# Attention: two places for the halves of normalised tiles and finished heads and for the output sum, and the heads' halves made one step later

## The chip, the cores and the metric

The kernel runs on one core of one Trainium2 chip. A core has a matrix engine (TensorE, PE in the profile; PEld are its weight loads), a vector engine (VectorE, DVE), a scalar engine (ScalarE, ACT), GpSimd (POOL) and a synchronisation engine (SyncE, SP), which issues every DMA of this kernel. Each engine works through its own queue in order and waits at semaphores for the others. SBUF is the on-chip memory of 128 partitions; addresses below are bytes within a partition. PSUM holds the sums of matmuls.

The metric is the device time of one execution in microseconds (us). A profiled execution gives the trace; its own time is given beside its span, which runs from the first to the last instruction.

## The reference

Two layers of a mixed network on a sequence of S = 2048 rows of D = 640. Each layer is an attention with a compressive memory followed by a gated mixing over the sequence; the same weights serve both layers.

```python
def A(x, wq, wk, wv, wo, beta):          # H = 32 heads of 20, N = 4 segments of 512 rows
    q, k, v = heads(x @ wq), heads(x @ wk), heads(x @ wv)
    for s in range(N):
        p = softmax(q[s] @ k[s].T * scale + causal_mask)
        a_mem = (phi(q[s]) @ M) / (phi(q[s]) @ z + 1e-6)
        o[s] = g * a_mem + (1 - g) * (p @ v[s])
        M, z = M + phi(k[s]).T @ v[s], z + phi(k[s]).sum()
    return concat(o) @ wo

def B(x, w_in, w_sp, b_sp, w_out):       # F = 1728
    z = gelu(x @ w_in); z1, z2 = z[:, :864], layernorm(z[:, 864:])
    return (z1 * (w_sp @ z2 + b_sp)) @ w_out

for _ in range(2):
    x = x + A(layernorm(x), ...)
    x = x + B(layernorm(x), ...)
```

## The kernel before

**Stages.** Per layer the kernel runs an attention (phase1a, class Attention), the projection into B with the rest of the attention's output projection (phase1b, "w_in stage"), and the mixing with the output projection of B (phase2 in the first layer, phase2s in the second). Every matmul works on halves: a float32 value is kept as a 16-bit high half and a 16-bit low half (the difference), and a product is three matmuls, high by high, high by low, low by high. Making halves is a copy on ScalarE for the high one and a subtraction for the low one.

**The attention in steps.** Heads are taken in 64 pairs per layer (16 per segment of 512 rows), and a pair takes three steps, c = 0, 1, 2. In a step PE computes a part of the scores of pair n (tile es, whose exponential on ScalarE is P) and of the transposed scores of pair n + 2 (tile mp, whose maxima on VectorE are mx). The casts that halve P (PH on ScalarE, PL on GpSimd, in the last four pairs partly on VectorE) are made in the steps c = 2 and c = 0, one head each, and the products of P with the values (pv) follow three steps later. combine, in a step c = 1, scales pv (rs, ab on VectorE) and adds its parts on GpSimd (oat). The maxima, turned by PE (mtp) and halved (mr), go by DMA into the rows of qk that the scores of a later step read. Between these steps PE works off "dense" jobs in a written order with paces: values (vps), queries and keys (qps, kps), and the output projection of finished tiles (yps).

post(k, f) runs f in the step k further on; that fixes where f's instructions stand in the program, and with it their priority.

**Finished heads.** Each segment has five units m of 6 or 8 heads. When the last pair of a unit has been combined, out() halves its 4 x 6 x 20 (or 4 x 8 x 20) columns: a copy on ScalarE (L1368), a subtraction on GpSimd (L1369), and two DMAs into o_d in DRAM (L1372). load_o brings such rows back transposed for project, and an assertion keeps its step behind the segment's last out().

**Normalised tiles.** prep loads a tile of x, normalises it in place (L1044), and halves and transposes it by DMA (split_t: L231 copy, L232 subtraction on GpSimd, L233 DMA transpose into xt). Its halves, named xnhl, take the same tag "xh" of the pool e1 as the heads' halves, named ohl: one place for both.

**The output sum.** project multiplies a transposed tile of heads by wo in two halves of 320 columns; for each, VectorE adds x and writes the sum x1 (L1104), and after the second the tile is stored (L1106). x1 has one place, tag "xn" of the pool e1. Twelve tiles a layer (0 to 11) go through project inside the attention, the last ones at its very end; tiles 12 to 15 are left to phase1b.

**Phase 1b** begins while the attention ends. For its first two tiles it loads x1 (L275), normalises it (tile xn, L225, after layernorm_stats), and halves and transposes it (tile xnhl, L231 to L233) into th, which the w_in matmuls (zp, L316) take. Tile i's matmuls with the second half of w_in come first, then those with the first half (wi0 in the first layer, loaded raw through the stages wst, L123, and split into wi0h and wi0l, L84 and L85; loaded ready in the second). xn and xnhl have one place each.

**Order.** Only PE's order is the program's own (manual_schedule). The other queues, SP's too, are laid out when the kernel is built, by a planner that simulates a timeline and takes the ready instruction of the highest priority.

**Memory.** Pools of one side are stacked in the order in which they are opened, and a later pool takes the bytes of an earlier one that has ended. With reuse_waits="tile" a tile in such a place waits only for those earlier tiles that held its own bytes, and for a tile that a DMA reads until that DMA has landed. In the program before, a partition is used as follows.

| bytes | the attention (left side) | first layer's phase1b, same bytes | second layer's phase1b (right side) |
|---|---|---|---|
| 83840-148288 | qk, vs, P, PH, PL, ot, gm, ab and others | zh, zl, z1, z2 | zb (left) |
| 148288-150848 | xh: xnhl and ohl (pool e1) | z2, xt | |
| 150848-153408 | xn: x1 (pool e1) | xt | o |
| 153408-158528 | xt, two places (e2) | xt, o, wst | o |
| 158528-163648 | bg, two places | wst | o, xt |
| 163648-171840 | phq, four places (u4) | wst, x1, th | xt, z2, zt |
| 171840-182080 | xt1 (ax) | th, xn, xnhl 176896-179456, wi0h from 179456 | z2, zt, z1 |
| 182080-182656 | small tiles, mr (al1); in the second layer mr alone, to 182592 | wi0h to 188096 | z1 to 183904 |
| above | free | wi0l 188096-196736 | xn 183904-186464, xnhl 186464-189024, x1, th to 199264 |

The pools of the attention that the change touches are opened in setup:

```python
sk, self.p3, self.pl2 = pool("ak", 1), pool("a3", 2), pool("al2", 2)
self.e1, self.e2, self.bg, self.u4, ax = pool("ae1", 1), pool("ae2", 2), pool("abg", 2), pool("au4", 4), pool("ax", 1)
self.pl1 = pool("al1", 1)
```

phase2 makes the first tiles of the second layer's attention ahead of it, with pools of its own under the same names (nxt.e2, nxt.e1).

Of the kernel before, what the change touches and what calls it, by code (L numbers as in the profile page):

```python
# [9 lines left out]
F32 = mybir.dt.float32  # L10
F32R = mybir.dt.float32r
F16 = mybir.dt.float16
# [7 lines left out]
S, D, H, DH, NSEG = 2048, 640, 32, 20, 4  # L20
# [606 lines left out]
def phase2(g, w_sp, x1_d, z1_d, zh, zl, out, nxt):  # L627
# [5 lines left out]
    with ExitStack() as ctx:  # L633
        pool = lambda n, b, **k: ctx.enter_context(tc.tile_pool(name=n, bufs=b, reuse_waits="tile", **k))
        right = lambda n, b: pool(n, b, side="right")
        p1, pr, ph0, ph1, p2, wp = pool("c1", 1), pool("cr", 1), pool("ch0", 1), pool("ch1", 1), pool("c2", 2), pool("cw", 1)
        sp, pt1, px, pt0 = right("cs", 3), right("ctr1", 1), right("cx", 1), right("ctr0", 1)
        nxt.e2, nxt.e1 = pool("ce2", 1), pool("ce1", 1)
        pg = pool("cg", 2, space=PSUM)
        py = pool("cy", 1, space=PSUM)  # L640
        nxt.pd = pool("cpd", 2, space=PSUM)
# [45 lines left out]
        def fetch(nm, src):  # L687
            o = p2.tile([128, src.shape[-1]], F32, tag=nm, name="c" + nm)
            nc.sync.dma_start(o, src)
            return o  # L690
# [54 lines left out]
        for t in range(NT):  # L745
# [8 lines left out]
            x1 = fetch("x1", x1_d[t])  # L754
# [102 lines left out]
def values_tile(g, pool):  # L857
    t = pool.tile([128, 4, H, 2 * DH + 1], F16, name="vs")
    g.nc.gpsimd.memset(t[:, :, :, DH:DH + 1], 1.0)
    return t  # L860
# [9 lines left out]
class Attention:  # L870
# [56 lines left out]
    def setup(self, ctx):  # L927
        g, nc, tc = self.g, self.nc, self.tc
        pool = lambda n, b, **k: ctx.enter_context(tc.tile_pool(name=n, bufs=b, reuse_waits="tile", **k))
        sk, self.p3, self.pl2 = pool("ak", 1), pool("a3", 2), pool("al2", 2)  # L930
        self.e1, self.e2, self.bg, self.u4, ax = pool("ae1", 1), pool("ae2", 2), pool("abg", 2), pool("au4", 4), pool("ax", 1)
        self.pl1 = pool("al1", 1)
        self.pd = pool("apd", 2, space=PSUM)
        self.px = pool("apx", 1, space=PSUM)
        self.pm = pool("apm", 1, space=PSUM)
        self.pe = pool("ape", 1, space=PSUM)
        self.po = pool("apo", 1, space=PSUM)
        self.qk = [sk.tile([128, 2, L], F16, name=f"qk{i}") for i in range(self.NQK)]
        self.vs[1] = values_tile(g, sk)
        self.xt[1] = ax.tile([128, 2, KD, L], F16, name="xt1")  # L940
# [90 lines left out]
    def prep(self, t, lead=False):  # L1031

        g, nc = self.g, self.nc
        s, c = t // 4, slice((t % 4) * 128, (t % 4) * 128 + 128)
        xt = self.e2.tile([128, D], F32, tag="xt", name="xt")
        nc.sync.dma_start(xt, self.x[t])
        ln = []

        def stats():
            ln.extend(layernorm_stats(g, xt, D, 2, XS))  # L1040

        def norm():
            mv, rs = ln
            nc.vector.tensor_scalar(xt, xt, mv[:, 0:1], rs, ALU.subtract, ALU.mult)  # L1044
            hl = self.e1.tile([128, 2, D], F16, tag="xh", name="xnhl")
            split_t(g, hl, self.xt[s % 2][:, :, :, c], xt, low=nc.gpsimd)

        def held(f):
            with self.tc.high_priority(offset=HP) if lead else self.hold():
                f()  # L1050

        return lambda: held(stats), lambda: held(norm)
# [30 lines left out]
    def project(self, t):  # L1083
        g, nc = self.g, self.nc
        wh, wl = g.wo.h, g.wo.l
        o = self.o.pop(t)
        oh, ol = o[:, 0], o[:, 1]
        xt = self.e2.tile([128, D], F32, tag="xt", name="xt")
        nc.sync.dma_start(xt, self.x[t])
        x1 = self.e1.tile([128, D], F32, tag="xn", name="x1")  # L1090
        yield 450
        for n in range(2):
            c = slice(n * 320, (n + 1) * 320)
            ps = self.pd.tile([128, L], F32, tag="dn", name="yps")[:, :320]
            i = 0
            for k in range(KD):
                for a, b in ((oh, wh), (oh, wl), (ol, wh)):
                    nc.tensor.matmul(ps, a[:, k, :], b[:, k, c], start=(i == 0), stop=(i == 14))  # L1098
                    i += 1
                    if i % 3 == 0:  # L1100
                        yield 3 * 136

            def out(ps=ps, c=c, n=n):
                nc.vector.scalar_tensor_tensor(x1[:, c], ps, g.yw, xt[:, c], ALU.mult, ALU.add)  # L1104
                if n:
                    nc.sync.dma_start(self.x1_d[t], x1)  # L1106

            self.post(1, out)
# [236 lines left out]
    def combine(self, n, s, m, h0):  # L1345
# [17 lines left out]

        def out():
            nh = len(UH[m])
            hl = self.e1.tile([128, 2, D], F16, tag="xh", name="ohl")[:, :, :4 * nh * DH].rearrange("p i (t h d) -> p i t h d", t=4, d=DH)
            oh, ol = hl[:, 0], hl[:, 1]
            nc.scalar.copy(oh, ot[:, :, :nh, :])  # L1368
            nc.gpsimd.tensor_tensor(ol, ot[:, :, :nh, :], oh, ALU.subtract)  # L1369
            c = slice(UH[m][0] * DH, (UH[m][0] + nh) * DH)  # L1370
            for i, o in enumerate((oh, ol)):
                nc.sync.dma_start(self.o_d[s][:, i, c].rearrange("(t p) c -> p t c", p=128), o.rearrange("p t h d -> p t (h d)"))  # L1372

        self.post(2, out)

    def run(self, nseg=NSEG):
        pairs = [(s, m, h0) for s in range(nseg) for m in range(NU) for h0 in UH[m][::2]]
# [227 lines left out]
```

## Time and profile before

| | us |
|---|---|
| median of three runs | 2323.73 (2322.91 to 2328.16) |
| the profiled execution's own time | 2331.88 |
| its span | 2330.2 |

By stages of the profiled execution (us from the start of the span; busy us of each engine):

| stage | from | to | PE | DVE | ACT | POOL | granted clock |
|---|---|---|---|---|---|---|---|
| start, first weights and tiles | 0 | 150 | 99.95 | 108.63 | 62.92 | 43.38 | 0.93 |
| first attention | 150 | 650 | 450.41 | 392.76 | 385.46 | 404.09 | 0.96 |
| into the w_in stage | 650 | 676 | 16.53 | 10.71 | 9.78 | 1.06 | 0.80 |
| w_in stage | 676 | 897 | 220.77 | 108.17 | 65.98 | 17.79 | 1.00 |
| mixing, first layer | 897 | 1250 | 352.89 | 158.48 | 71.75 | 13.68 | 1.00 |
| into the second attention | 1250 | 1300 | 44.87 | 29.57 | 18.23 | 6.11 | 0.97 |
| second attention | 1300 | 1790 | 457.42 | 385.28 | 396.44 | 422.62 | 0.99 |
| w_in stage | 1790 | 1983 | 191.79 | 130.84 | 71.99 | 59.94 | 1.00 |
| mixing, second layer | 1983 | 2330 | 338.85 | 178.94 | 91.78 | 2.85 | 1.00 |

How to read the lines of the profile: a group has line, engine, operation, tiles as out<-in, count, then busy us, mean ns of one, idle us of the engine just before them and what ended that idle time. A line of the timeline has start and duration in us, engine, line, operation and tiles, a count, and in brackets the idle time before it with its releaser. SPq is SP's queue at the issue of a DMA. A line of waits has the waiting instruction, what it waited for, us in total, times, and the longest. A line of windows has the stretch, its length, the busy time of PE, PEld, DVE, ACT and POOL with the number of instructions, the granted clock of PE, the share of the DMA engines that was busy, and GB/s.

### The profile page before, as it was taken

To read this page: it belongs to the slowest core of one execution; us is meant where nothing else is said; L and a number is where in the kernel's file an instruction comes from. 1 tells how busy PE (TensorE), PEld (TensorE's weight loads), DVE (VectorE), ACT (ScalarE), POOL (GpSimd) and SP (SyncE) were. 2 spreads that over 40 slices of the span, in tenths; PEclk is the share of its full clock that TensorE was granted. 3 is DMA by queue.
4 is the path that set the end of the run, shared out by engine and by line. 5 is a ranking of instruction groups with operands and counts; after the bars stand their busy time and mean duration, and the time that the engine had idled before them with its cause. 6 is when DMAs were issued, how large, how long until landed. Compare 5 with 4: busy or idle time off the path is not lost.

```text
span 2330.2 us, 50381 instructions
## 1 busy us (share of the span) xinstructions
PE 2173.5 (93%) x20490; PEld 1297.3 (56%) x20490; DVE 1503.4 (65%) x2791; ACT 1174.3 (50%) x1452; POOL 971.5 (42%) x726
## 2 busy tenths in 40 slices
PE   4878899899889999999999989999998999999998
PEld 2445465556645555555655555656665555555655
DVE  8678868877644545454434788787776757555454
ACT  3279778787632232122212797887875324322221
POOL 2178778888710000000001688888895323000000
PEclk9999899999999999999999999999999999999999
DMA  5654544544563457878655336354466434977875
GB/s 162 166 138 102 131 107 128 129 144 117 146 168 90 132 160 196 244 189 243 162 144 157 75 92 181 103 125 95 122 170 166 116 102 102 264 205 188 227 200 124
DMA packets 509561, 350.16 MB, mean 150 GB/s; under 512 B 409296, under 2 KB 444496, under 8 KB 504208
## 3 DMA queue, kind: packets, MB, share of 16 engines
q1 hardware_dynamic: 509328, 346.93, 56.4%
q8 instruction: 161, 2.64, 0.5%
q14 instruction: 72, 0.59, 0.1%
HBM read 160.83 MB, written 97.93 MB: 111 GB/s over the span
## 4 chain that ended last, share of the span: by engine, by line
PE 65%; DVE 11%; DMA 8%; ACT 7%; issue 3%; SPq 1%; POOL 1%; ACTq 0%; DVEq 0%; POOLq 0%
PE zp L316 14%; PE gp L683 10%; PE pv L1341 4%; PE cyp L715 3%; PE yps L1098 3%; PE cyp L519 3%; DVE mx L1304 3%; PE ga L469 3%; PE mp L1288 3%; PE kps L1122 3%; ACT P L1297 2%; PE qps L1122 2%; PE vps L1065 2%; PE gb L469 2%; ACT PH L1314 2%
## 5 line engine op out<-in xcount | busy, mean ns | idle before, releaser
L1315 POOL TENSOR_TENSOR PL<-P,PH 128x1280 f16<-128x1280 f32 x248 | 649.5, 2621 | 167.8 <-ACT PH L1314 154.7
L1304 DVE TENSOR_REDUCE mx<-mp 128x2 f32<-128x1024 f32 (+3 forms) x512 | 408.8, 818 | 97.2 <-PE mp L1260 95.6
L1297 ACT ACTIVATE P<-es,sc 128x1024 f32<-128x1024 f32 (+1 forms) x384 | 370.3, 964 | 135.3 <-PE es L1260 133.2
L1314 ACT CAST PH<-P 128x1280 f16<-128x1280 f32 x256 | 320.4, 1253 | 21.6 <-PE pv L1341 12.9
L219 POOL TENSOR_TENSOR lnrs<-lnve,mhalf 128x1 f32<-128x1 f32 x92 | 56.1, 618 | 576.2 <-DVE lnve L218 576.2
L316 PEld LDWEIGHTS <-th 128*128 128x128 f16 x1920 | 188.5, 98 | 177.2 <-issue 16.4
L683 PE MATMUL gp<-zh,wt 128*128 128x432 f16 x1024 | 231.4, 346 | 0.3 <-DMA wt<-wn 0.3
L683 PEld LDWEIGHTS <-wt 128*128 128x128 f16 x1536 | 150.1, 98 | 129.8 <-DMA wt<-wn 1.1
L1288 PEld LDWEIGHTS <-qk 60*128 60x128 f16 (+1 forms) x2048 | 91.1, 93 | 225.8 <-issue 154.3
L469 PEld LDWEIGHTS <-wt 128*128 128x128 f16 x1344 | 131.5, 98 | 112.6
L1288 PE MATMUL mp<-qk 60*128 60x512 f16 (+3 forms) x1024 | 138.2, 307 | 41.1 <-DVE mx L1304 40.1
L1341 PE MATMUL pv<-vs,PH 128*128 128x41 f16 x2560 | 168.6, 183 | 2.1 <-DVE ab L1357 2.0
L1260 PEld LDWEIGHTS <-big 64*128 64x128 f16 x3072 | 141.5, 96 | 50.9 <-issue 3.9
L1341 PE MATMUL pv<-vs,PL 128*128 128x41 f16 x2560 | 164.4, 182 | 4.4 <-POOL PL L1315 3.9
L1288 PE MATMUL es<-qk 64*128 64x512 f16 (+3 forms) x1024 | 135.7, 300 | 35.0 <-ACT P L1297 25.4
L1065 PE MATMUL vps<-wvh,xt 128*128 128x320 f16 x640 | 151.5, 302 | 3.6 <-DVE vs L1071 3.0
L1341 PEld LDWEIGHTS <-PH 128*128 128x128 f16 x2560 | 142.9, 96 | 18.7
L316 PE MATMUL zp<-wi1h,th 128*128 128x432 f16 x640 | 149.2, 348 | 2.1 <-DVE x L1104 1.3
L1341 PEld LDWEIGHTS <-PL 128*128 128x128 f16 x2560 | 143.4, 97 | 7.8 <-POOL PL L1315 4.7
L683 PE MATMUL gp<-zl,wt 128*128 128x432 f16 x512 | 135.3, 346 | 0.0
L1122 PE MATMUL kps<-xt,wkh 128*128 128x512 f16 x380 | 124.0, 395 | 9.1 <-DVE phl L1156 9.0
L696 DVE TENSOR_TENSOR u<-u,cz 128x864 f32<-128x864 f32 x16 | 17.0, 1060 | 160.8 <-ACT u L694 120.4
(253 smaller groups left out, 4386.2 us busy)
## 6 DMA issues: line engine op xcount, KB each, us to landing
wr<-in_B_w_sp_dram SPq DMA_DIRECT2D x32, 1024.0 KB
qk<-st SPq DMA_DIRECT2D x256, 120.0 KB
x<-x SPq DMA_DIRECT2D x56, 320.0 KB
z<-z SPq DMA_DIRECT2D x32, 432.0 KB
cz<-z SPq DMA_DIRECT2D x32, 432.0 KB
turned<-wt SPq DMA_DIRECT2D x24, 512.0 KB
wt<-turned SPq DMA_DIRECT2D x24, 512.0 KB
st<-qhl SPq DMA_DIRECT2D x40, 256.0 KB
```

The lines of the kernel that those rows point to most:

```text
L316: nc.tensor.matmul(zp[:, n, :FHH], a[:, k, :], b[:, k, c:c + FHH], start=(k == 0 and j == 0), stop=(k == KD - 1 and j == 2))
L469: nc.tensor.matmul(o[:, :FHH], wt[:, x, m, :], zb[b][:, y, m, :], start=start and i == j == 0, stop=i == NP - 1 and j == 2, skip_group_che ...
L683: nc.tensor.matmul(gp[:, n, :FHH], ready[t][:, k % 2, a, k // 2, :], b[:, k, n * FHH:(n + 1) * FHH], start=(i == 0 and j == 0), stop=(i == ...
L1065: nc.tensor.matmul(ps, a[:, k, c], b[:, k, n * 320:(n + 1) * 320], start=(i == 0), stop=(i == 14))
L1122: nc.tensor.matmul(ps, a[:, k, c], b[:, k, :], start=(i == 0), stop=(i == 14))
L1260: nc.tensor.matmul(out, g.big[r, 64 - 64 * s:192 - 64 * s], mk, start=False, stop=s == 1, skip_group_check=True)
L1288: nc.tensor.matmul(out[:, h, o:o + w], a[r, ac], b[r, bc], start=o == 0, stop=False, skip_group_check=True)
L1297: self.last_of["ACT"] = nc.scalar.activation(P[:, :, 512 * c:512 * c + ew], es[:, :, :ew], AF.Exp, scale=g.esc).ins
L1304: self.last_of["DVE"] = nc.vector.tensor_reduce(self.mx[m][:, :, i], mp[:, :, o:o + w], AX.X, ALU.max).ins
L1314: nc.scalar.copy(PH, P[:, h])
L1315: (nc.gpsimd if h == 0 or n < self.N - self.TAIL else nc.vector).tensor_tensor(PL, P[:, h], PH, ALU.subtract)
L1341: nc.tensor.matmul(pv[:, i, h, :], x[:, c:c + 128], v[:, j, h0 + h, :], start=(j == 0 and x is PH), stop=(j == i and x is PL), skip_group_ ...
```

## The change

The pool e1 of one place goes. The halves of normalised tiles and of finished heads get a pool axh of two places, still shared by both, and the output sum x1 gets a pool axn of two places; both are opened last, behind al1. In phase2 the pool of one place that prep uses there gets the new name. The halves of finished heads are posted three steps on instead of two, but for the last pair of the layer, which keeps two.

```diff
-        nxt.e2, nxt.e1 = pool("ce2", 1), pool("ce1", 1)
+        nxt.e2, nxt.xh = pool("ce2", 1), pool("ce1", 1)
...
-        self.e1, self.e2, self.bg, self.u4, ax = pool("ae1", 1), pool("ae2", 2), pool("abg", 2), pool("au4", 4), pool("ax", 1)
-        self.pl1 = pool("al1", 1)
+        self.e2, self.bg, self.u4, ax = pool("ae2", 2), pool("abg", 2), pool("au4", 4), pool("ax", 1)
+        self.pl1, self.xh, self.xn = pool("al1", 1), pool("axh", 2), pool("axn", 2)
...
-            hl = self.e1.tile([128, 2, D], F16, tag="xh", name="xnhl")
+            hl = self.xh.tile([128, 2, D], F16, tag="xh", name="xnhl")
...
-        x1 = self.e1.tile([128, D], F32, tag="xn", name="x1")
+        x1 = self.xn.tile([128, D], F32, tag="xn", name="x1")
...
-            hl = self.e1.tile([128, 2, D], F16, tag="xh", name="ohl")[:, :, :4 * nh * DH].rearrange("p i (t h d) -> p i t h d", t=4, d=DH)
+            hl = self.xh.tile([128, 2, D], F16, tag="xh", name="ohl")[:, :, :4 * nh * DH].rearrange("p i (t h d) -> p i t h d", t=4, d=DH)
...
-        self.post(2, out)
+        self.post(2 if n + 1 == self.N else 3, out)
```

A place of either tag is 2560 bytes (2 x 640 values of 16 bits, or 640 of 32 bits).

## The prediction

> **What bounds the kernel now.** The page comes first, then the waits of TensorE (PE) in each attention stage, then the stages' windows.
>
> ```profile
> span 2330.2 us, 50381 instructions
> PE 2173.5 (93%) x20490; PEld 1297.3 (56%) x20490; DVE 1503.4 (65%) x2791; ACT 1174.3 (50%) x1452; POOL 971.5 (42%) x726
> PE es L1288 <- ACT P L1297: 11.6, 9, 3.5
> PE es L1288 <- DMA qk<-mr: 4.5, 3, 2.1
> PE pv L1341 <- POOL PL L1315: 1.6, 3, 1.1
> PE es L1288 <- ACT P L1297: 11.7, 16, 1.8
> PE es L1288 <- DMA qk<-mr: 4.0, 4, 1.7
> 1790.00:1983.00 193.00, 191.79 (x1081) 105.69 (x1081) 130.84 (x227) 71.99 (x104) 59.94 (x62) 1.00 0.44 118
> ```
>
> PE is the bound: 93% of the span, and 191.8 of 193 us in the w_in stage behind the second attention (1790 to 1983). Its order is written out, so a hole in PE is lost unless a later hole shrinks by it. The three rows of waits from 150 to 650 us and the two from 1300 to 1780 us (us, times, longest) say what this change can touch: 11.6 + 11.7 = 23.3 us for ScalarE's P, 8.5 us for the maxima's DMA. VectorE's maxima make longer holes; the change leaves them.
>
> **What it does in the attention.** Halves of normalised tiles (xnhl) and of finished heads (ohl) share one place now, so each waits for the other's DMA.
>
> ```profile
>   DMA xt<-xnhl: 9.4, 6
>   DMA xt<-xnhl: 12.7, 5
> L1369 POOL TENSOR_TENSOR ohl<-oat,ohl x40: 1091/1098/1403, 152.8 to 1789.5; 128x480 f16<-128x480 f32 x32, 128x640 f16<-128x640 f32 x8
> 413.29 0.72 ACT L1368 CAST ohl<-oat 128x640 f16<-128x640 f32 x1 [1.88 <-DMA xt<-xnhl]
> 417.44 0.28 PE L1288 MATMUL es<-qk 64*128 64x256 f16 x2 [2.74 <-ACT P L1297]
> 1559.71 0.72 ACT L1368 CAST ohl<-oat 128x640 f16<-128x640 f32 x1 [1.17 <-DMA xt<-xnhl]
> 1563.86 0.29 PE L1288 MATMUL es<-qk 64*128 64x256 f16 x2 [1.80 <-ACT P L1297]
> 197.37 0.59 ACT L1368 CAST ohl<-oat 128x480 f16<-128x480 f32 x1
> 199.03 0.40 PE L1288 MATMUL es<-qk 64*128 64x384 f16 x4 [1.29 <-ACT P L1297]
> 1390.56 0.28 PE L1288 MATMUL es<-qk 64*128 64x256 f16 x2 [1.30 <-ACT P L1297]
> 201.72 0.69 ACT L1297 ACTIVATE P<-es,sc 128x512 f32<-128x512 f32 x1 [0.46 <-PE es L1260]
> ```
>
> The first row is ScalarE's (ACT's) wait ahead of ohl for the other's transpose, the second the same ahead of xnhl. The second place takes away both, 9.4 + 12.7 = 22.1 us of ACT. PE feels few of them: at 413.29 the wait and the copy, 1.88 + 0.72 = 2.6, are nearly all of PE's 2.74; at 1559.71 they are 1.89, all of its 1.80. One step later ohl also leaves the step in which ACT has exponentials, a PH cast and mr: the pattern of 197.37, a copy of 0.59 just ahead of a P for which PE then waits 1.29, occurs four times (199.03 is the first, 1390.56 the last), worth about 4 x 0.6 = 2.4. Together 2.6 + 1.8 + 2.4 = 6.8. Bounds: the whole 23.3 gained; or, where the copy now stands ahead of the third P, in which ACT idles 0.46, 0.59 - 0.46 = 0.13 lost on each of 38 moved copies, 4.9. I take **-6**, by the rows that show the coupling.
>
> Moved with it go POOL's subtraction and two DMA issues, 38 times. On POOL it goes behind the next pair's sums (oat), ahead of the next PL; PE waits only 1.6 us for PL in 500, so PL's lead of three steps hides it. Without that cover it would cost 1.10 x 38 = 42. On the DMA queue the issues now come after the step's mr instead of ahead of it: nothing to 8.5 gained, taken as 0. The o store lands a step (about 2.6 us) later; the earliest read of it is held three steps further back by the assertion in front of load_o. Behind each moved wait of SP stand qk fetches, as before.
>
> The second place for the sum x1 removes a wait of VectorE (DVE) for the previous store:
>
> ```profile
> L1104 DVE SCALAR_TENSOR_TENSOR x<-yps,sc,xt 128x320 f32<-128x320 f32 x48 | 25.9, 540 | 15.0 <-PE yps L1098 7.4 <-DMA x<-x 5.5 <-PE pv L1341 1.7
> 645.26 0.32 SPq L1106 DMA_DIRECT2D x<-x  x1
> 647.49 0.55 DVE L1104 SCALAR_TENSOR_TENSOR x<-yps,sc,xt 128x320 f32<-128x320 f32 x1 [0.94 <-DMA x<-x]
> 1778.25 0.53 SPq L1106 DMA_DIRECT2D x<-x  x1
> 1781.53 0.55 DVE L1104 SCALAR_TENSOR_TENSOR x<-yps,sc,xt 128x320 f32<-128x320 f32 x1 [0.78 <-DMA x<-x]
> ```
>
> Bounds -5.5 to 0. The last sum of each attention waits for PE itself, so I take **-1**. In phase 2 the pool is only renamed, one place as before: 0, with nothing to cover.
>
> **What it does at the end of the second attention.** Here the change adds a wait. The pools stack from byte 83840. Without ae1, everything from ae2 on slides down by 5120; al1 then ends at 177472 (second layer), axh at 182592, and x1's two places are 182592-185152 and 185152-187712. Phase 1b's right-hand pools don't move: xn lies at 183904-186464, xnhl at 186464-189024. In the program before, the attention ended at 182592, below both. Now the first xn lies on both x1 places, and can be written only when the last two sums (tiles 10 and 11) have been stored.
>
> ```profile
> 1771.77 0.59 DVE L225 TENSOR_SCALAR xn<-x,lnmv,lnrs 128x640 f32<-128x640 f32 x1
> 1772.39 0.73 ACT L231 CAST xnhl<-xn 128x640 f16<-128x640 f32 x1
> 1773.15 0.83 DVE L232 TENSOR_TENSOR xnhl<-xn,xnhl 128x640 f16<-128x640 f32 x1
> 1774.53 1.32 SPq L233 DMA_TRANSPOSE th<-xnhl  x1
> 1779.10 0.72 ACT L231 CAST xnhl<-xn 128x640 f16<-128x640 f32 x1 [0.24 <-DMA th<-xnhl]
> 1790.42 76.81 PE zp L316 x420
> 1790.48 0.43 SPq L1106 DMA_DIRECT2D x<-x  x1
> 1791.48 1.32 SPq L421 DMA_DIRECT2D wr<-in_B_w_sp_dram  x2
> 1792.86 0.54 SPq L1372 DMA_DIRECT2D o<-ohl  x1
> 1803.31 1.25 SPq L281 DMA_TRANSPOSE o<-o  x1
> ```
>
> The first xn is made at 1771.77 now, 18.7 us ahead of the matmuls (zp, 1790.42) that need its transpose. Then it would begin after the store of 1790.48 lands. Fast end: store 2.23 (645.26 to 647.49), 0.59, 0.73, 0.83, transpose 4.57 (1774.53 to 1779.10): 8.95, so zp at 1799.4, **9.0** late. Slow end: store 3.28 (1778.25 to 1781.53) and 2.15 of halves put the transpose at 1795.9, behind two loads of wr (1 MB each) and the low half of ohl; that half, issued at 1792.86, released the o<-o transpose only at 1803.31. A transpose behind it lands by 1803.31 + 4.57 = 1807.9, **17.5** late. The nearest row is that ohl store, same queue and same microseconds, so I take 13.5, a little above the middle. Queued on PE behind zp is the whole w_in stage, full at 191.8 of 193, so nothing absorbs it. Behind xn on DVE, and behind xnhl on ACT, stands work on z, which needs zp itself.
>
> The Trainium skill ("DMA: Bandwidth & Descriptors", Queues, rings and completion order) says that each DMA engine takes descriptors in ring order. The ohl row agrees; by that rule the transpose starts after wr and ohl, and the delay is nearer 14 than 9.
>
> After the stall PE is slower for a while, as at the first layer's stall:
>
> ```profile
> 664.88 0.88 PE L316 MATMUL zp<-wi0h,th 128*128 128x432 f16 x2 [6.90 <-ACT wi0h L84]
> 665.00:675.00 10.00, 7.87 (x25) 3.08 (x24) 6.00 (x7) 4.31 (x5) 0.00 (x0) 0.67 0.66 237
> ```
>
> After a hole of 6.90 the granted clock was 0.67 over 7.87 us of work: 0.33 x 7.87 = 2.6 lost. Bounds 0 to 2.6; I take 1.5. The boundary costs **+15**.
>
> The Trainium skill ("TensorE: Matmul & The Clock Gate", What's actually happening) has the array at half clock after an idle window of about 3.4 us until a busy one; an estimate by that page is 0.5 x 3.4 = 1.7.
>
> **At the end of the first attention** wi0h (179456-188096) now lies on both ohl and both x1 places; the stages for it (wst) move off the last sums' tiles onto older ones.
>
> ```profile
> 650.72 0.50 SPq L1106 DMA_DIRECT2D x<-x  x1
> 653.22 1.02 ACT L84 ACTIVATE wi0h<-wst,iv 128x864 f16<-128x864 f32 x1 [4.78 <-DMA wst<-in_B_w_in_dram]
> 656.93 1.33 SPq L281 DMA_TRANSPOSE o<-o  x1
> 658.39 0.96 SPq L123 DMA_DIRECT2D wst<-in_B_w_in_dram  x2
> ```
>
> PE waits here for wi0 until after 670 whatever comes first. The first two loads wait for the last sum's tiles now. If they leave earlier, ohl and x1 land by about 650.72 + 3.28 = 654.0, the split starts 0.8 later than 653.22, and the third load leaves about 2 us ahead of 658.39, no longer behind o<-o (656.93): -3 with the clock. If not, the split waits to 656.9 and the third load to about 659: +1.5. I take **-1**.
>
> **Sum**: 15 - 1 - 6 - 1 = +7, on the profiled 2331.88 (span 2330.2) 2338.9. The median shown is 2323.73, 8.15 lower; the holes are the same kind there, so **2330.7**.
>
> **Rivals.** (1) The transpose slips past the loads: 9.0 and no clock loss, so 9 - 1 - 6 - 1 = +1, 2324.7. For it the 4.57 of 1774.53, against it 1803.31. (2) Faster: ACT's relief reaches every pair, since PE's order couples all steps, and the 23.3 us for P go: 15 - 1 - 23.3 - 1 = -10.3, 2313.4; it decides from 17.7 of relief. Against it, most of those holes have no ohl beside them. (3) The relief is nothing and the moved copy pays its 4.9, the first boundary its 1.5, x1 gains nothing: 15 + 1.5 + 4.9 = +21.4, 2345.1. For it, the planner lays out every queue but PE's anew. (4) The change's new wait doesn't arise, because the places land elsewhere: -1 - 6 - 1 = -8, 2315.7.
>
> **Chances**: forecast 0.37 (own range 2326 to 2336), rivals 0.26, 0.12, 0.18, 0.07. A difference under 0.2% (4.65 us) can't be told from none. Faster: 0.12 + 0.07 and a little of (1), 0.20. Within: most of (1) and the low end of the forecast, 0.28. Slower: 0.52. Leaving out the far parts of (2) and (3), the range is 2316 to 2341.
>
> **What would show it.** The first xn of the second layer near 1794 instead of 1772, waiting for a DMA of x; zp 9 to 17 us behind the last yps, with a dip in the clock; the waits of ACT for xt<-xnhl gone; PE's 23.3 us for P at about 17. It is wrong if zp follows yps at once, or if P's waits fall below 6 us.

## The result and the profile after

| | median us | ratio to before, 95% interval |
|---|---|---|
| before, four runs | 2325.06 (2322.91 to 2328.16) | |
| after, four runs | 2349.19 (2344.45 to 2353.18) | 1.0103 (1.0088 to 1.0117) |

The change costs 24 us. One execution of xh_last_xn_low, 3279 us at a granted clock of 0.62, stands apart from its other eleven (2319 to 2330) and is left out of its ratio. The profiled execution of after took 2349.28 (span 2347.6); that of before, 2331.88, lay above its median, so profile against profile shows only 17.4. A second profile of the kernel before (below, before_again; span 2319.9) is therefore used beside the first wherever a few us matter.

The page and the waits of TensorE (PE) and ScalarE (ACT) come first. The first two rows of waits are of 150 to 643 us, the next three of 1300 to 1796, the last of ACT from 109 to 1796 (us in total, times, longest).

```profile
span 2347.6 us, 50366 instructions
PE 2172.5 (93%) x20490; PEld 1296.9 (55%) x20490; DVE 1504.4 (64%) x2791; ACT 1174.4 (50%) x1452; POOL 971.0 (41%) x726
```

```profile
PE es L1288 <- ACT P L1297: 7.0, 9, 1.9
PE kps L1122 <- DVE phl L1156: 4.9, 1, 4.9
...
PE mp L1288 <- DVE mx L1304: 15.6, 20, 2.8
PE es L1288 <- ACT P L1297: 10.1, 11, 3.3
PE es L1288 <- DMA qk<-mr: 2.9, 2, 1.9
...
ACT xnhl L231 <- DMA xt<-xnhl: 3.2, 1, 3.2
```

No engine is busier than before by more than 1.0 us. PE waits 7.0 + 10.1 = 17.1 us for P instead of 23.3, and of ACT's 9.4 + 12.7 us for the other's transpose (over the whole execution) 3.2 are left. That is what the change set out to do. But PE's first attention now has one hole (idle time) of 4.9 us for phl, halves made from the keys (kps); their making stands behind a normalisation on VectorE (DVE).

The end of the second attention, in the timeline (start, duration, engine, line; in brackets the idle time before and what ended it):

```profile
1796.53 0.32 SPq L1106 DMA_DIRECT2D x<-x  x1
1796.95 0.87 SPq L421 DMA_DIRECT2D wr<-in_B_w_sp_dram  x2
1797.87 0.45 SPq L1372 DMA_DIRECT2D o<-ohl  x1
...
1799.10 0.61 DVE L225 TENSOR_SCALAR xn<-x,lnmv,lnrs 128x640 f32<-128x640 f32 x1 [2.60 <-DMA x<-x]
1799.74 0.72 ACT L231 CAST xnhl<-xn 128x640 f16<-128x640 f32 x1 [4.14 <-DVE xn L225]
...
1801.35 3.75 SPq L233 DMA_TRANSPOSE th<-xnhl  x1
...
1807.90 0.90 PE L316 MATMUL zp<-wi1h,th 128*128 128x432 f16 x2 [11.99 <-DMA th<-xnhl]
```

The ten us behind it, in the view by windows (busy us of PE, PEld, DVE, ACT and POOL, the granted clock, the DMA share, GB/s):

```profile
1808.00:1818.00 10.00, 10.00 (x45) 4.86 (x45) 2.25 (x4) 2.94 (x3) 0.00 (x0) 0.80 0.83 137
```

xn waits for the store of x1, issued at 1796.53. The transpose leaves 4.8 us after that store was issued and lands at 1807.90, and PE stands still for 11.99 us. With the granted clock at 0.80 over the ten us behind that, 0.20 x 10 = 2.0 us more are lost.

The end of the first attention:

```profile
641.20 0.73 ACT L1368 CAST ohl<-oat 128x640 f16<-128x640 f32 x1 [5.83 <-POOL oat L1360]
649.52 1.92 ACT L84 ACTIVATE wi0h<-wst,iv 128x864 f16<-128x864 f32 x2 [7.59 <-DMA xt<-in_A_x_dram]
651.35 0.71 ACT L231 CAST xnhl<-xn 128x640 f16<-128x640 f32 x1
...
659.25 0.90 PE L316 MATMUL zp<-wi1h,th 128*128 128x432 f16 x2 [17.02 <-DMA th<-xnhl]
```

The first halves of the next phase (xnhl) had been made before the last copy of the heads' halves, in the first profile of before at 631.01:

```profile
631.01 0.72 ACT L231 CAST xnhl<-xn 128x640 f16<-128x640 f32 x1 [0.21 <-DVE xn L225]
...
647.72 0.73 ACT L1368 CAST ohl<-oat 128x640 f16<-128x640 f32 x1 [5.83 <-POOL oat L1360]
```

Now they come at 651.35, behind two splits of wi0 in ACT's queue, and zp begins after a hole of 17.02 us, where PE had begun at once and waited 6.90 and a few short times inside zp.

And a third place that the prediction had not looked at, the start of the second attention:

```profile
1258.21 0.94 SPq L1036 DMA_DIRECT2D xt<-x  x2
1269.52 1.01 PE L1122 MATMUL kps<-xt,wkh 128*128 128x512 f16 x2 [4.18 <-DVE phl L1156]
1280.18 0.42 PE L1065 MATMUL vps<-wvh,xt 128*128 128x320 f16 x1 [3.10 <-DVE vs L1071]
```

PE waits there for phl and for vs, the halves of the values, both made on DVE. Before, the same rows left earlier and the same two holes were 2.44 and 1.06:

```profile
1241.09 0.85 SPq L1036 DMA_DIRECT2D xt<-x  x2
1269.40 1.01 PE L1122 MATMUL kps<-xt,wkh 128*128 128x512 f16 x2 [2.44 <-DVE phl L1156]
1278.04 0.30 PE L1065 MATMUL vps<-wvh,xt 128*128 128x320 f16 x1 [1.06 <-DVE vs L1071]
```

From the start of the last product of the first mixing to the first P of the second attention, first before, then after, then a kernel with the next phases' tiles moved (after_xnhl_free, below), the view by windows has:

```profile
1257.56:1292.09 34.53, 30.43 (x197) 15.03 (x195) 19.05 (x31) 9.91 (x17) 4.73 (x4) 0.95 0.59 141
1255.93:1297.02 41.09, 33.18 (x197) 15.86 (x195) 22.12 (x41) 9.78 (x18) 5.92 (x6) 0.88 0.54 135
1249.13:1286.73 37.60, 31.15 (x197) 15.13 (x195) 22.07 (x41) 9.89 (x18) 5.92 (x6) 0.91 0.58 147
```

Of the 6.6 us by which the stretch grew, 3.8 are idle time of PE; the other 2.8 are the same 197 matmuls taking longer, at a granted clock of 0.88 instead of 0.95.

For all kernels the span can be cut at rows that every profile has. A runs from the first P (L1297) of the first attention to its last copy of heads' halves (L1368); B from there to the start of the last product of the first mixing (cyp, L715); C to the first P of the second attention; D to its last copy of halves; E to the first zp (L316); F to the end. Before A lie 109 to 114 us.

| us | A | B | C | D | E | F |
|---|---|---|---|---|---|---|
| before, first profile | 535.7 | 609.8 | 34.5 | 496.6 | 1.7 | 539.7 |
| before, second profile | 530.4 | 605.5 | 34.9 | 497.2 | 1.7 | 537.0 |
| after | 531.8 | 614.7 | 41.1 | 497.9 | 13.0 | 539.6 |
| order_only | 532.6 | 614.7 | 40.3 | 497.1 | 1.7 | 536.5 |
| post_only | 538.4 | 607.2 | 33.8 | 499.3 | 1.7 | 537.1 |
| places_only | 535.3 | 613.4 | 39.9 | 497.1 | 13.0 | 539.7 |
| places_front | 526.2 | 614.4 | 37.2 | 497.7 | 1.7 | 536.0 |
| after_xn_low | 527.9 | 615.5 | 40.2 | 498.2 | 1.7 | 539.4 |
| xh_last | 529.9 | 609.8 | 36.0 | 496.3 | 21.6 | 541.0 |
| xh_last_xn_low | 528.4 | 608.8 | 37.1 | 496.9 | 1.7 | 536.6 |
| xh_last_xn_low_old_step | 531.7 | 610.8 | 35.9 | 498.8 | 1.7 | 536.7 |
| both_new_step | 527.7 | 608.7 | 35.8 | 497.6 | 1.7 | 536.5 |
| both_old_step | 533.1 | 609.2 | 36.4 | 497.0 | 1.7 | 537.6 |
| after_both_low | 525.4 | 617.8 | 40.5 | 499.0 | 1.7 | 539.1 |
| after_xnhl_free | 528.0 | 609.3 | 37.6 | 496.5 | 1.7 | 537.2 |
| xnhl_free_xt_back | 526.3 | 608.8 | 36.8 | 497.7 | 1.7 | 538.7 |
| swap_single | 530.9 | 606.0 | 34.3 | 496.9 | 1.7 | 536.9 |

After against the mean of the two profiles of before: A -1.2, B +7.1, C +6.4, D +0.9, E +11.3, F +1.3, and -3.2 ahead of A; together +22.6, close to the 24 of the medians. The loss sits in B, C and E, the three handovers between phases. A of one and the same kernel differs by 5.3, so a single profile says nothing about 3 us in A.

### The profile page after: what moved, and what is told of

It is laid out like the page before. It is cut to its first block, busy times and chain, and to the rows that moved or that the text cites. A ratio compares the mean times of both kernels' runs of the same rounds, so it can differ in the third digit from the quotient of the medians.

```text
span 2347.6 us, 50366 instructions
## 1 busy us (share of the span) xinstructions
PE 2172.5 (93%) x20490; PEld 1296.9 (55%) x20490; DVE 1504.4 (64%) x2791; ACT 1174.4 (50%) x1452; POOL 971.0 (41%) x726
## 5 line engine op out<-in xcount | busy, mean ns | idle before, releaser
L1297 ACT ACTIVATE P<-es,sc 128x1024 f32<-128x1024 f32 (+1 forms) x384 | 370.4, 965 | 140.6 <-PE es L1260 138.6
L316 PEld LDWEIGHTS <-th 128*128 128x128 f16 x1920 | 189.0, 99 | 195.4 <-DMA th<-xnhl 30.7
L316 PE MATMUL zp<-wi1h,th 128*128 128x432 f16 x640 | 151.5, 352 | 29.6 <-DMA th<-xnhl 29.6
```

What stands on the lines that cost most here:

```text
L316: nc.tensor.matmul(zp[:, n, :FHH], a[:, k, :], b[:, k, c:c + FHH], start=(k == 0 and j == 0), stop=(k == KD - 1 and j == 2))
L1297: self.last_of["ACT"] = nc.scalar.activation(P[:, :, 512 * c:512 * c + ew], es[:, :, :ew], AF.Exp, scale=g.esc).ins
```

## The experiments

"Theory" was, from the first set on: nothing is lost by the second places or by the later step as such; the loss is where the pools, opened in a new order, come to lie against the phases before and behind.

**order_only.** One place each and the old step; only the order of the pools is the changed kernel's.

```diff
-        self.e1, self.e2, self.bg, self.u4, ax = pool("ae1", 1), pool("ae2", 2), ...
-        self.pl1 = pool("al1", 1)
+        self.e2, self.bg, self.u4, ax = pool("ae2", 2), pool("abg", 2), ...
+        self.pl1, self.e1 = pool("al1", 1), pool("ae1", 1)
```

> One place each, step as before; only the order in which the pools are opened is the changed kernel's, so the single places of the halves and of x1 lie last (177,472 to 182,592 in the second attention) and the xt rows lie first, at 148,288. Theory (the loss is where the places lie): the second attention starts about 6 us late as in the changed kernel (xt rows loaded near 1258 instead of 1241), the first attention's end costs about 6 (the splits of wi0 wait for the last stores of halves and x1), the second attention's end costs nothing, since the next phase's xn at 183,904 lies on none of the two places; no relief: 2337 us, 2331 to 2342. Rival 1 (the loss comes with the second places or the later step, not with the order): 2325, 2321 to 2328. Rival 2 (only the second attention's end matters): 2325 too, with zp there on its old distance and xt rows loaded at 1241.

Measured 2337.79, ratio 1.0061 (1.0046 to 1.0076).

```profile
656.86 0.71 ACT L231 CAST xnhl<-xn 128x640 f16<-128x640 f32 x1
...
664.65 0.90 PE L316 MATMUL zp<-wi1h,th 128*128 128x432 f16 x2 [17.31 <-DMA th<-xnhl]
...
1263.74 0.93 SPq L1036 DMA_DIRECT2D xt<-x  x2
...
1800.07 0.53 PE L316 MATMUL zp<-wi1h,th 128*128 128x432 f16 x2 [0.64 <-DVE x L1104]
```

The late halves with the hole of 17.31 at the first end and the late rows of xt are all there, and the second end is whole, as foretold. So the new order alone costs 0.6%, in B and C; what the second places add is E, because only with them does x1 reach the bytes of xn.

**post_only** is the kernel before with the later step alone; **places_only** is the changed kernel with the old step.

```diff
-        self.post(2, out)
+        self.post(2 if n + 1 == self.N else 3, out)
```

> The old places, one each, and only the heads' halves one step later. Theory: none of the three late starts (xt rows at 1241 in the second attention, zp 0 to 1 us behind the last yps at both ends); of the relief only the part that stands on the order of copy and P, not the waits for the halves' place, which stay: 2321, 2316 to 2326. Rival 1 (the whole relief is the later step): 2316 to 2318. Rival 2 (the later step costs by itself, because the one place is now held longer and the next xnhl waits for it): 2328 to 2335, with ACT's waits for xt<-xnhl longer than before.

> The changed kernel with the halves made at the old step. Theory (places where they lie cost about 23 at three spots, the relief of some 6 comes from the two changes together): 2351, 2346 to 2356. Rival 1 (the relief is the second places alone): 2349, 2347 to 2351, with the first attention as short as in the changed kernel (last yps near 642). Rival 2 (the later step causes part of the loss): 2340 or less.

Measured: post_only 2325.64, ratio 1.0007 (0.9995 to 1.0019); places_only 2351.41, ratio 1.0125 (1.0105 to 1.0145). With one place the step gains nothing, less than the 4 that the theory gave it. With the places but not the step the loss stays.

**places_front.** Two places and the later step; the halves' places first, x1's between bg and u4.

```diff
-        self.e2, self.bg, self.u4, ax = pool("ae2", 2), pool("abg", 2), pool("au4", 4), pool("ax", 1)
-        self.pl1, self.xh, self.xn = pool("al1", 1), pool("axh", 2), pool("axn", 2)
+        self.xh, self.e2, self.bg, self.xn = pool("axh", 2), pool("ae2", 2), pool("abg", 2), pool("axn", 2)
+        self.u4, ax, self.pl1 = pool("au4", 4), pool("ax", 1), pool("al1", 1)
```

> The changed kernel, two places each and the later step, but the pools opened so that the halves' two places begin at 148,288, xt and o stand where they stood before the change, x1's two places follow at 163,648, and what is free early lies last. Theory (the loss is where the places lie): none of the three late starts; the relief of 6 to 7 in the attentions stays: 2318, 2313 to 2323. Rival 1 (the second places or the later step cost by themselves): 2340 to 2350. Rival 2 (x1's two places under the next phase's rows at 164,096 only move the wait of the first attention's end): 2322 to 2328, with the rows' first loads after 644.

Measured 2328.87, ratio 1.0021 (1.0008 to 1.0034): rival 2 in its mechanism, 0.9 us above its range. Most of the loss is gone, E wholly, but B is still 614.4:

```profile
637.32 0.32 SPq L1106 DMA_DIRECT2D x<-x  x1
639.60 0.80 SPq L275 DMA_DIRECT2D x<-x  x2
...
654.30 0.90 PE L316 MATMUL zp<-wi1h,th 128*128 128x432 f16 x2 [17.61 <-DMA th<-xnhl]
```

Now the next phase's rows lie under x1's places, their load leaves only after the last store of x1, and zp is as late as in the changed kernel, by another chain.

**after_xn_low.** The changed kernel; only in the phase behind the second attention are xn and its halves moved, to 164,896.

```diff
-            pe2, pe1, p2, p1, px2, px1, sp = right("be2", 2), right("be1", 1), right("b2", 2), right("b1", 1), ...
+            pe2, p2, p1, pe1, px2, px1, sp = right("be2", 2), right("b2", 2), right("b1", 1), right("be1", 1), ...
```

> The changed kernel with one thing more: in the phase after the second attention xn and its halves lie at 164,896 to 170,016 instead of 183,904 to 189,024, so on none of x1's or the halves' places; nothing else of the attention moves. Theory (the second attention's end costs 11.3 us, because xn waits for the stores of x1): zp 1 to 2 us behind the last copy of the halves as before the change, the late xt rows and the first attention's end as in the changed kernel: 2349.2 less 11.3 is 2338, 2333 to 2343. Rival 1 (the transpose queues behind the loads of the next phase's weights whatever xn does): 2345 to 2350. Rival 2 (the freed z tiles at 182,112 to 189,024 wait for x1's places in their turn): 2340 to 2346 with a hole after the first zp.

Measured 2330.69, ratio 1.0040 (1.0028 to 1.0053). That lies below the expected range in us, but the kernel before ran 3.5 us faster in this set than in that of the result (2321.54 against 2325.06); as a ratio, 2333 to 2343 is 1.0034 to 1.0077, and the run lies inside.

```profile
1773.52 0.76 DVE L225 TENSOR_SCALAR xn<-x,lnmv,lnrs 128x640 f32<-128x640 f32 x1
...
1793.86 0.53 PE L316 MATMUL zp<-wi1h,th 128*128 128x432 f16 x2 [0.64 <-DVE x L1104]
```

xn is made 20 us ahead of zp again. From 1.0103 to 1.0040 are 0.63% of 2322, 14.6 us, for this one wait (10 to 19 by the two intervals). In the profiles E falls by 11.3, and in that of after the clock behind the hole had taken 2.0 more.

**xh_last** puts x1's places at 148,288, leaves xt and o where they were before the change, and only the halves' places last. **xh_last_xn_low** adds the move of after_xn_low.

```diff
-        self.e2, self.bg, self.u4, ax = pool("ae2", 2), pool("abg", 2), pool("au4", 4), pool("ax", 1)
-        self.pl1, self.xh, self.xn = pool("al1", 1), pool("axh", 2), pool("axn", 2)
+        self.xn, self.e2, self.bg, self.u4, ax = pool("axn", 2), pool("ae2", 2), pool("abg", 2), pool("au4", 4), pool("ax", 1)
+        self.pl1, self.xh = pool("al1", 1), pool("axh", 2)
```

> The changed kernel, but x1's two places at 148,288, xt and o where they stood before the change, and only the halves' two places last, at 182,592 to 187,712 (182,656 to 187,776 in the first attention). Theory: xt rows load at their old time (near 1241, the 6 us gone); at the first attention's end the splits of wi0 wait for the last stores of the halves, some 5 us, which is no later than they came before the change, and xn and its halves are free, so zp begins within 2 us and nothing is lost; at the second attention's end xn lies on the halves' places and waits for their last stores instead of x1's, 11 to 13 us late: 2338, 2333 to 2343. Rival 1 (only x1 under xn costs at the second end): 2326, 2322 to 2330. Rival 2 (the splits of wi0 on the halves' places are what costs 5 at the first end): 2343.

> The last two together: x1's places at 148,288, the halves' places last, and in the phase after the second attention xn and its halves at 164,896. Two places each and the later step, and nothing that is needed early on a place that comes free late. Theory (all of the loss was in the three late starts, and the relief of ScalarE in the attentions buys nothing, since other waits of TensorE take its place): 2326, 2322 to 2330. Rival 1 (the relief of 4 to 6 us is real and the late starts hid it): 2319 to 2322. Rival 2 (the later step or the second places cost by themselves): 2331 to 2336.

Measured: xh_last 2346.46, ratio 1.0107 (1.0094 to 1.0120); xh_last_xn_low 2323.42, ratio 1.0008 (0.9998 to 1.0019). B is 609.8, so the first end costs nothing here, though the splits of wi0 lie on the halves' places. The second end missed its range: 19.9 us late instead of 11 to 13.

```profile
1784.28 1.03 SPq L421 DMA_DIRECT2D wr<-in_B_w_sp_dram  x2
1785.35 0.49 SPq L1372 DMA_DIRECT2D o<-ohl  x1
...
1795.29 0.61 DVE L225 TENSOR_SCALAR xn<-x,lnmv,lnrs 128x640 f32<-128x640 f32 x1 [12.08 <-DMA o<-ohl]
...
1803.14 0.90 PE L316 MATMUL zp<-wi1h,th 128*128 128x432 f16 x2 [20.52 <-DMA th<-xnhl]
```

The store of the halves was issued just behind the loads of wr and freed xn 9.9 us later; x1's store, in the profile of after, was issued just ahead of such loads (1796.53 against 1796.95) and freed xn after 2.6. The Trainium skill ("DMA: Bandwidth & Descriptors", Queues, rings and completion order) has each DMA engine take descriptors in ring order; these two rows agree with it. That the stores of halves are slow as such is ruled out by the first profile of before: without such loads in front, two of them (416.46 and 1562.87) let the next xnhl begin 2.3 and 2.9 us after their issue.

**swap_single.** The kernel before, with the single places of x1 and the halves exchanged.

```diff
-        self.e1, self.e2, ... = pool("ae1", 1), pool("ae2", 2), ...
+        self.e1x, self.e1, self.e2, ... = pool("ae1x", 1), pool("ae1", 1), pool("ae2", 2), ...
...
-        x1 = self.e1.tile([128, D], F32, tag="xn", name="x1")
+        x1 = self.e1x.tile([128, D], F32, tag="xn", name="x1")
```

> The kernel before the change, one place each and the old step, with the two places exchanged: x1 at 148,288 and the halves at 150,848, so that the first halves of the second attention's start no longer lie on the last u of the mixing (146,176 to 149,760) and need not wait for its last product. Theory: these halves are of tiles that come into use only later, so they come 8 us earlier (near 1250 instead of 1257.9) and nothing else moves: 2326, 2323 to 2329. Rival (they stand in the queues of ScalarE and of the transposes ahead of the first heads, and what is early there is early in all): 2318 to 2322.

Measured 2325.37, ratio 1.0010 (1.0001 to 1.0019), C 34.3: those early halves are of no use, as the theory had it.

**after_both_low** was to settle the first end: after_xn_low, and in the phase behind the first attention xn and its halves below x1 and th.

```diff
-            pe2, pe1, wp0 = pool("be2", 2), pool("be1", 1), pool("bw0", 1)
+            pe1, pe2, wp0 = pool("be1", 1), pool("be2", 2), pool("bw0", 1)
```

> The changed kernel with xn and its halves at 164,896 after the second attention, as in the run before, and in the phase after the first attention the same exchange: xn and its halves at 164,096 to 169,216 (on the heads' scores and xt1, free early), x1 and th above them. The splits of wi0 still lie on the halves' and x1's places. Theory (what made the first zp late was not the splits of wi0 themselves, but that the first halves of the next phase, at 176,896 to 179,456, lay on the halves' place at 177,536 and so came behind those splits on ScalarE): zp within 2 us of the last copy of the halves, the stretch from there to the mixing's last product 609 to 611 instead of 615, and 4.9 us less than with xn low in the second phase alone: ratio 1.0019, 1.0005 to 1.0030. Rival (the splits on places that come free late are the cost): ratio stays at 1.0040.

Measured 2332.61, ratio 1.0043 (1.0030 to 1.0056). It tells nothing on the question, since something else came late:

```profile
635.47 0.72 ACT L1368 CAST ohl<-oat 128x640 f16<-128x640 f32 x1 [5.83 <-POOL oat L1360]
...
640.22 1.52 SPq L275 DMA_DIRECT2D x<-x  x2
...
647.41 1.66 DVE L216 BATCH_NORM_STATS2 lnst<-x 128x6 f32<-128x320 f32 x4
...
657.27 0.90 PE L316 MATMUL zp<-wi1h,th 128*128 128x432 f16 x2 [20.75 <-DMA th<-xnhl]
```

The rows of x1, whose place this edit moved too, were loaded only 4.8 us after the last copy of halves.

**after_xnhl_free** keeps xn low after the second attention, and after the first it takes only the halves of the next phase out, to 194,176, above wi0 (wi0 slides down by their 2,560 bytes and still lies on all four places).

```diff
-            pe2, pe1, wp0 = pool("be2", 2), pool("be1", 1), pool("bw0", 1)
+            pe2, pe1, wp0, pe1h = pool("be2", 2), pool("be1", 1), pool("bw0", 1), pool("be1h", 1)
...
-            hl = pe1.tile([128, 2, D], F16, tag="xnhl", name="xnhl")
+            hl = (pe1h if w0 is None else pe1).tile([128, 2, D], F16, tag="xnhl", name="xnhl")
```

> The changed kernel with xn low after the second attention and, in the phase after the first attention, nothing moved but the one place of the next phase's halves: at 194,176, which nothing of the attention uses, instead of 176,896, of which 1,920 bytes lie on the heads' halves' first place (wi0 moves down by 2,560 and still lies on all four places). Theory (the first attention's end costs 4 to 5 us because these halves lie on the heads' halves' place, and so come behind the splits of wi0 on ScalarE): the first halves come before the last copy, zp within 2 us of it, the stretch from there to the mixing's last product 609 to 611, ratio 1.0019, 1.0005 to 1.0032. Rival (the splits of wi0 on places that come free late are the cost): zp early all the same but the stretch stays at 615, ratio 1.0035 to 1.0050.

Measured 2321.85, ratio 0.9997 (0.9987 to 1.0007), below the expected range.

```profile
623.63 0.72 ACT L231 CAST xnhl<-xn 128x640 f16<-128x640 f32 x1
639.82 0.72 ACT L1368 CAST ohl<-oat 128x640 f16<-128x640 f32 x1 [5.83 <-POOL oat L1360]
...
641.50 0.52 PE L316 MATMUL zp<-wi1h,th 128*128 128x432 f16 x2 [0.64 <-DVE x L1104]
...
650.11 1.92 ACT L84 ACTIVATE wi0h<-wst,iv 128x864 f16<-128x864 f32 x2 [9.56 <-DMA o<-ohl]
```

The splits still wait 9.56 us for the stores of the halves, and it doesn't matter: xnhl is made 16 us ahead of the last copy, zp follows at once, B is 609.3. So at the first end it was the 1,920 bytes that xnhl shared with the heads' halves. The step from 1.0040 to 0.9997 is 10 us (6 to 14 by the two intervals). Of these B gives 6.2 and C 2.6; C fell too, with the second attention's places unmoved. Against after_xn_low (33.10 busy of 40.20) PE is busy 1.95 less for the same matmuls (31.15 of 37.60), at a granted clock of 0.91 instead of 0.87, and idle 0.65 less. The hole for vs is 1.5 instead of 3.0, and the second drop of the clock, which stands behind that hole in after_xn_low, is not there. Why vs came earlier was not taken apart.

The rows of xt still leave as late here as in the changed kernel (1251.35, 2.2 behind the start of the mixing's last product). So the whole 24 us are back with the third overlap still in place.

**both_new_step and both_old_step**: xh_last_xn_low with the later and with the old step, in one set. The old step had been tried before, in another set than the new one, as **xh_last_xn_low_old_step**: 2330.31, ratio 1.0038 (1.0025 to 1.0052), its rival 1.

> Two places each where nothing waits for them (x1's at 148,288, the halves' last, xn low in the phase after the second attention), but the halves made at the old step, so only the later step is taken back. Theory (the copy's place in ScalarE's queue is worth nothing, since other waits of TensorE take its place): the same as with the later step, ratio 1.0008, 0.9990 to 1.0025. Rival 1 (the later step helps with two places): 1.0025 to 1.0045. Rival 2 (the later step hurts): 0.9970 to 0.9990.

> Two places each where nothing waits for them, the halves one step later: the run of xh_last_xn_low again, beside the same kernel with the old step. Theory A (the later step is worth nothing): both 1.0008 to 1.0038 with intervals that overlap by half. Theory B (with two places the later step is worth 0.3%): 1.0008, 0.9995 to 1.0020.

> The same kernel with the halves at the old step. Theory A: within 0.1% of both_new_step. Theory B: 0.25% to 0.4% above it.

Measured: new 2324.04, ratio 1.0004 (0.9995 to 1.0012); old 2331.68, ratio 1.0037 (1.0024 to 1.0050). Theory B: with two places the later step is worth 0.33%, and without it two places alone cost that much. In the profiles it is mostly A, 527.7 against 533.1. PE's waits for P (112 to 640) are only 2.3 of that, first the new, then the old step:

```profile
PE es L1288 <- ACT P L1297: 8.6, 10, 1.7
```

```profile
PE es L1288 <- ACT P L1297: 10.9, 10, 3.3
```

Over A by windows, in the same order:

```profile
111.20:638.90 527.70, 471.90 (x6652) 301.26 (x6652) 421.15 (x814) 411.10 (x517) 427.13 (x285) 0.97 0.50 129
110.60:643.70 533.10, 475.95 (x6652) 303.56 (x6652) 420.44 (x814) 411.08 (x517) 427.60 (x285) 0.96 0.49 127
```

PE's idle time falls by 1.35 (55.80 against 57.15); the other 4.05 are the same 6652 matmuls, which take less time at the higher granted clock.

**xnhl_free_xt_back** exchanges the places of o and xt in after_xnhl_free, so that xt lies where it did before the change; **before_again** is the kernel before.

```diff
-        self.e2, self.bg, self.u4, ax = pool("ae2", 2), pool("abg", 2), pool("au4", 4), pool("ax", 1)
+        self.bg, self.e2, self.u4, ax = pool("abg", 2), pool("ae2", 2), pool("au4", 4), pool("ax", 1)
```

> The kernel of after_xnhl_free with one thing more: the places of o (148,288) and of the xt rows (153,408) exchanged, so that the rows of the second attention's first tiles no longer lie on the last u of the mixing. All three late starts are then gone, with two places each and the later step. Theory: rows loaded near 1240 instead of 1258; of the 3.1 us by which the second attention's first P still came late there (37.6 against 34.5 behind the mixing's last product) 0.5 to 2 go, the rest is two transposes in a row ahead of the first heads' transfers: ratio 0.9990, 0.9978 to 1.0003. Rival (the rows' late load had no cost left): 0.9997 as before, 0.9990 to 1.0010.

> The kernel before the change, unchanged, as one more profile of it, since its one profile (2331.9) lies above the median of its runs. Theory A (the relief in the first attention is real: 528 us from the first P to the last copy with two places and the later step, 532 to 533 with the old step, 535.7 before): first attention 533 to 537 again, second 496 to 498, ratio 1.0000. Theory B (535.7 was that one execution's): first attention 527 to 531.

Measured: xnhl_free_xt_back 2322.58, ratio 0.9999 (0.9990 to 1.0009), C 36.8 for 37.6, so the rows' late load had no cost left that a time can show (the rival; the measured ratio lies in both ranges); before_again 2322.45, ratio 1.0004 (0.9993 to 1.0015), A 530.4: theory B, 535.7 was that one execution's.

No version is faster than the kernel before; the best of the changed ones can't be told from it.

## Why the prediction was wrong

The direction was right, the size was not: +7 was foretold, +24 came. By its own steps:

**End of the second attention, +15** (13.5 and 1.5 for the clock): right in its mechanism. xn waited for a DMA of x, 2.57 us behind the issue of that store (1796.53) where 2.23 to 3.28 were given; the transpose stood behind wr and ohl and landed 6.55 us after its issue, 2.0 more than the 4.57 of the fast end and far less than the slow end had it; zp came 11.3 later than before in E, inside 9.0 to 17.5, and the clock took 2.0. Together that is 13.3, 1.7 under the term. Taking the cause away gave back 14.6.

**End of the first attention, -1**: this step failed. It said "PE waits here for wi0 until after 670 whatever comes first", and weighed only wi0h against the new places. The table of memory ahead of it had the next phase's xnhl at 176,896 to 179,456, and the new places of the halves begin at 177,536. That xnhl lost its lead of 16 us and zp began after a hole of 17.02; that wi0 was ready by then took back only a part: B +7.1, and 10 by the run that frees xnhl. The prediction held xn and xnhl against the new places in the second layer, and not in the first.

**Phase 2, "only renamed, one place as before: 0"**: this step failed too. Taking ae1 out from under ae2 slid the xt rows 5120 bytes down, onto 148,288. There lies ut, the turned u of the mixing (146,176 to 149,760), which the mixing's last product reads. The rows left at 1258.21, just behind that product, instead of 1241.09. In the profile C grows by 6.4, more by idle time (3.8 of 6.6 against the first profile) than by a lower clock (2.8); order_only, with no second place at all, has the same 40. So the new order of the pools is enough for that loss, and the sum had no term for it, because the prediction followed the moved pools into the phases behind and never into the phase ahead. That the late rows alone make the 6.4 is not shown: in after_xnhl_free they are as late, and C is 37.6; with the rows early it is 35.8 to 37.2.

**Relief in the attentions, -6, and x1, -1**: the waits went as said, 17.1 us for P where "about 17" stood; VectorE's 7.4 us ahead of the sums for a DMA of x are gone. But the 7 us of the two terms are not in the time: the step that failed here is the one that counted a wait taken away as time won. Over the nine profiles with two places and the later step, A averages 528.0; over the four with one place each and the old step (before twice, order_only, swap_single), 532.4. So about -4.4 in the first attention. Hardly any of it is a shorter wait: PE's idle time in A is 56.1 on average over the nine and 56.5 over the four, so other holes took the place of those for P. What fell is the time that the same 6652 matmuls take, 471.8 against 475.9: 469.4 to 473.2 over the nine, 474.1 to 478.2 in every profile with the old step, 478.0 in post_only. The granted clock was 0.968 on average against 0.963, which is about 2.6 of these 4.1. Why the clock is higher there, and what the rest is, isn't shown. D is +0.5 in the second, 497.5 against 497.0; in the profile of after PE waits there 15.6 for mx instead of 11.7. The versions with nothing late give the 4 back: B 608.9 (xh_last_xn_low, both_new_step, after_xnhl_free, xnhl_free_xt_back) against 607.1 (the four named, without order_only), +1.8; C 36.8 against 34.6, +2.2; -4.4, +0.5, +1.8 and +2.2 make +0.1. The 0.5 and the 1.8 are within what the two profiles of before differ by (D 496.6 and 497.2, B 609.8 and 605.5). What is late in C there is seen in both_new_step and its like: two xnhl are made in a row, their two transposes stand together (2.94 us of SP's queue at 1252.15) ahead of the first heads' transfers, and ScalarE's phl behind them waits 2.25 us for such a transfer (st<-qhl), where it waited 1.18 before. Rival 3, "the relief is nothing", was the nearest in its result, 2345.1 against the 2349.2 measured, but that is luck, its cause wasn't there: the moved copy doesn't pay 4.9, it earns 0.33% once there are two places, and the first boundary cost 10 and not 1.5.

Rivals 1, 2 and 4 fell: the transpose did not slip past the loads, P's waits did not vanish, and the new wait did arise.

What stays open: why the same matmuls take less time in the first attention with two places and the later step; why two places with the old step cost 0.37%, when A is no longer with them (533.4 over three profiles) than with one (532.4); and what in the planner's new order of DVE made vs earlier in after_xnhl_free.

## What to carry to other kernels

When a pool moves in a stack, every tile above it moves too, and each must be held against the phase ahead (what is read last there) as well as the phase behind (what is written first), layer by layer: two overlaps, of 2,560 and 1,920 bytes, cost 14.6 and 10 us here by the runs that take them away, while the second places themselves, with the later step, cost nothing that the times can tell (ratio 0.9997). A buffer that comes free late belongs under something that is needed late; an engine's queue in front of it tells what will be held up with it. A wait that is taken off an engine beside the bound one is worth what the bound engine's holes lose in sum, not what the one row loses: here the row for P lost 4.6 us in the first attention (11.6 to 7.0), and the sum 0.4 on average. Busy time of the same matmuls in two profiles tells apart what idle time and what the granted clock has done.

## What the runs showed of the hardware that was not expected

One and the same program gave A of 535.7 and 530.4 us in two executions, and times from 2315.96 to 2328.91 in one set of 23: 0.56%, against the 0.2% that was taken as the least difference that can be told from none. A store issued 1.1 us behind two weight loads freed its bytes after 9.9 us, one issued 0.4 us ahead of two such loads after 2.6. After the hole of 11.99 us the granted clock was 0.80 over ten us, 2.0 us lost; the Trainium skill ("TensorE: Matmul & The Clock Gate", What's actually happening) has half clock until a busy window of about 3.4 us has passed, by which an estimate is 1.7, and the trace agrees. Behind the hole of only 3.10 us at 1280.18 in after, the granted clock was 0.69 from 1280 to 1290: 3.1 us lost, more than that estimate; behind the hole of 1.06 in the first profile of before (1278.04) it was 1.00 from 1278 to 1288.
